# Scales of q and k taken from each job's own tiles, and the load of f issued first

## The chip, the cores and the metric

The kernel runs on one core of a Trainium2 chip. The metric is the device time of one execution in microseconds (us), lower is better. The unchanged kernel took 1197.27 us, the median of three runs that lay between 1194.51 and 1199.98 us.

## What is computed

The reference is an attention with a decay, followed by a feed-forward layer. The inputs are q, k, v of shape (8 batches, 8 heads, 576 positions, 64), f of shape (8, 8, 576), w_in of 512 x 2048 and w_out of 2048 x 512, all float32.

```python
scores = matmul(q, k.T) / sqrt(64)
cum = cumsum(log(clip(f, 1e-4, 1)), axis=-1)
scores = where(causal, -1e9, scores + cum[..., :, None] - cum[..., None, :])
attn = softmax(scores)                       # max subtracted, sum + 1e-9
x = matmul(attn, v)                          # laid out as 4608 tokens x 512
h = x @ w_in
g = where(h >= 1, h, where(h <= -1, 0, (h + 1) ** 2 / 4))
out = g @ w_out
```

## The kernel before

Float32 products are made of float16 ones: a value is scaled by a power of two and split into a high and a low float16 part, and three matmuls (high-high, high-low, low-high) stand for one product. The scale has to be known before the split, and it is taken from the largest absolute value of the data.

**Jobs.** The attention is cut into 36 jobs, numbered p = 0 to 35. A job is one batch and one pair of heads. Batch 0 is cut once more by rows, so jobs 0 to 3 are the first 256 positions of batch 0 and jobs 4 to 7 the rest; jobs 8 to 11 are batch 1, and so on, four jobs a batch. Jobs 0 to 11 score in float32, and jobs 12 to 35 (`NQK` is 12) score with the split of q and k. A job goes through these steps:

- `load` (L340) brings q and k of the pair into one of two float32 tiles `qk32` by DMA, two jobs ahead of their use.
- `load_decay` (L369) brings rows of the running sums of log f, `cum_d`, into `ck`.
- `prepare` (L379) makes the transposed q and k. For jobs from 12 on ScalarE (L389) and VectorE (L390) write the high and low parts `qs`, and one DMA transpose (L393) turns them into `qkT`.
- `scores` (L443) runs the score matmuls of one row block into the PSUM tile `s` (L466), and GpSimd (POOL) builds the decay term from `ck`, `nsig` and `cqs` (L474, L478).
- `weights` (L542) joins the two on VectorE (L556), runs the exponential on ScalarE (L560) and the normalisation and split on both (L574, L575), and transposes the result by DMA (L581).
- `values` (L588, L595) multiplies by v and writes the batch's x (L605); jobs 0 to 7 use `early_values` (L529, L537).

**Feed-forward units.** There are 18 chunks of 256 tokens times 8 blocks of the hidden layer, 144 units. A unit is `moe_front` (matmuls L637, then ScalarE and VectorE L646 to L651) and `moe_back` (matmuls L665). A unit can run when its tokens are finished. The main loop deals the units that are ready over the row blocks of the next jobs; what is left at the end runs by itself.

**Weights.** `weight_load` and `weight_split` (L177, L189) bring the feed-forward weights in and split them, among jobs 1 to 6. The split is mostly VectorE work (L196, L199, L202, L228).

**Scales.** `across(dst, m)` (L111) spreads the largest value over all partitions: a PE transpose of the 128 x n tile into `s` (L119), three VectorE operations (L121, L122, L126), a small PE matmul with ones (L129) and a copy back (L130). `scale_of` (L105) makes the power of two with three VectorE operations (L107, L101, L109). The PSUM tile `s` has one buffer, which the score matmuls and `across` share.

- `value_scale(b)` (L236) reads v of a batch a second time, four DMAs on POOL's queue into the tile `vm` (two buffers), each followed by a VectorE maximum (L245), then one `across`.
- `query_scale(b)` (L261) does the same for q and k of a batch: eight DMAs of 288 KB on POOL's queue (L268) into the same two `vm` buffers, eight maxima (L269), one `across`, and then `nsig`, `nalpha` and `cqs` (L278 to L284). It is called for batches 2 to 7, six times.

**What sets the order.** Instructions are recorded in the order of the program, and a scheduler then puts them into the five engines' queues by what it takes to be ready. Each queue runs strictly in its order. Work whose inputs are there early, such as the maxima of `query_scale`, is moved far ahead of the place where it is written: the 48 loads of `query_scale` stand in the trace between 18.5 and 371.8 us.

**Start.** `load(0)`, then `decay_sums` (L140): the load of f (L143), the logarithm, the running sum, its store to `cum_d` (L153), from which the `ck` rows are loaded (L372).

Of the kernel before, what the change touches and what calls it, by code (L numbers as in the profile page):

```python
# [8 lines left out]
F32 = mybir.dt.float32  # L9
# [6 lines left out]
P = 128  # L16
# [14 lines left out]
NQK = 12  # L31
# [14 lines left out]
def kernel(  # L46
# [90 lines left out]
    cum_d = dram.tile([B * H, S], F32, name="cum_d")  # L137
    cq8 = const.tile([P, NT5, B * H], F32, name="cq8")

    def decay_sums():  # L140
        fl = early
        nb = B * H
        nc.sync.dma_start(fl[0:nb, 0:S], f.rearrange("b h s -> (b h) s"))  # L143
# [112 lines left out]
    sqk = const.tile([P, 2, B], F32, name="sqk")  # L256
    nsig = const.tile([P, B], F32, name="nsig")
    nalpha = const.tile([P, B], F32, name="nalpha")
    cqs = [const.tile([P, NT5, H], F32, name=f"cqs{i}") for i in range(2)]

    def query_scale(b):  # L261

        ms = tiny.tile([P, 2, NPAIR], F32, name="m8", bufs=2)
        for j, src in enumerate((q, k)):
            for i in range(NPAIR):
                st = two.tile([P, S], F32, name="vm")
                part = src[b, 2 * i:2 * i + 2].rearrange("h s d -> (h s d)").rearrange("(p n) -> p n", p=P)
                nc.gpsimd.dma_start(st, part)  # L268
                nc.vector.tensor_reduce(  # L269
                    out=ms[:, j, i:i + 1], in_=st, axis=AX.X, op=ALU.max, apply_absolute_value=True  # L270
                )
        m2 = tiny.tile([P, 2], F32, name="m2q", bufs=2)
        nc.vector.tensor_reduce(out=m2, in_=ms, axis=AX.X, op=ALU.max)
        mk = tiny.tile([P, 2], F32, name="mk", bufs=2)
        across(mk, m2)
        sc = sqk[:, :, b]
        scale_of(sc, mk, mk)
        nc.vector.tensor_scalar(  # L278
            out=nsig[:, b:b + 1], in0=sc[:, 0:1], scalar1=sc[:, 1:2], scalar2=-8.0, op0=ALU.mult, op1=ALU.mult
        )  # L280
        nc.vector.reciprocal(nalpha[:, b:b + 1], nsig[:, b:b + 1])
        nc.vector.tensor_scalar(
            out=cqs[b % 2], in0=cq8[:, :, b * H:(b + 1) * H], scalar1=nsig[:, b:b + 1], scalar2=-0.125,
            op0=ALU.mult, op1=ALU.mult,  # L284
        )

    early_z = const.tile([P, 5, NB], F32, name="early_z")

    class Scales:
# [89 lines left out]
    def prepare(w):  # L379

        t_ = two.tile([P, 2, 2, SP], F16, name="qkT")
        if w.p >= NQK:
            w.nsig, w.nalpha = nsig[:, w.b:w.b + 1], nalpha[:, w.b:w.b + 1]
            w.cqs = cqs[w.b % 2][:, :, 2 * w.hp:2 * w.hp + 2]
            w.qk = [(t_[:, 0, lq], t_[:, 1, lk]) for lq, lk in ((0, 0), (0, 1), (1, 0))]
            qs = one.tile([P, 2, 2, SP], F16, name="qs")
            for j in range(2):
                sc = sqk[:, j, w.b:w.b + 1]
# [348 lines left out]
    for p in range(njobs + 1):  # L737
# [3 lines left out]
        if w:  # L741
# [82 lines left out]
```

## Time and profile before

| | |
|---|---|
| time, median of 3 | 1197.27 us |
| the profiled execution | 1195.69 us |
| its span, first to last instruction | 1193.9 us |
| mean granted TensorE clock | 0.951 |
| PE (TensorE matmul) busy | 1064.8 us, 89% |
| DVE (VectorE) busy | 806.8 us, 68% |
| ACT (ScalarE) busy | 770.4 us, 65% |
| POOL (GpSimd) busy | 476.1 us, 40% |

The profile is of one execution. PEld is the load of matmul weights. The page gives the busy time of each engine over the whole span; other views give the same for any stretch of it, list the instructions of an engine in order of time with the idle time before each and what ended it, and add up the waits between pairs of lines. A row of a timeline reads: start in us, duration in us, engine, line, operation, output and inputs, shapes, count, and in brackets the idle time before it and the releaser. Instructions on an engine's own sequencer that only issue DMAs carry a q (SPq).

### The profile page before, as it was taken

The numbers are of one execution on the slowest core, as the hardware profiler recorded it, in microseconds if no ns is written. First come the engines' busy times: TensorE is split into PE (matmuls) and PEld (weight loads), VectorE is DVE, ScalarE is ACT, GpSimd is POOL, SyncE is SP. The second block draws the span as 40 slices with busy tenths as digits, with TensorE's granted clock in tenths as the row PEclk, the third lists the DMA queues.
The fourth block names the chain that finished last, engine by engine and source line by source line (L and its number), as shares of the span: only waits on it lengthen the run. The fifth ranks groups of instructions, "written<-read, shape, count | busy, mean of one in ns | idle before, by whom it ended". The sixth has DMA issues, their size and how long they took to land. (4 is left out here: it accounts for less than half of the span.)

```text
span 1193.9 us, 24608 instructions
## 1 busy us (share of the span) xinstructions
PE 1064.8 (89%) x8871; PEld 681.6 (57%) x8871; DVE 806.8 (68%) x2140; ACT 770.4 (65%) x1599; POOL 476.1 (40%) x811
## 2 busy tenths in 40 slices
PE   2566766998689899999999999999999999999998
PEld 1334443655356556655666665565566666677665
DVE  5979878777778777768656666777767866522222
ACT  2756555758567767777667666786777776644443
POOL 3588643534464544544432232454434444000000
PEclk9767888999789999999999999999999999999999
DMA  8797744689989977867665555777767773300000
GB/s 269 220 296 210 216 138 143 134 192 162 181 159 201 188 132 161 153 137 147 123 115 103 108 111 116 149 157 139 141 129 146 128 130 66 74 19 2 19 18 18
DMA packets 392537, 162.60 MB, mean 136 GB/s; under 512 B 370016, under 2 KB 371040, under 8 KB 392416
## 3 DMA queue, kind: packets, MB, share of 16 engines
q1 hardware_dynamic: 377312, 115.03, 49.4%
q0 software_dynamic: 9920, 36.58, 10.8%
q10 hardware_dynamic: 5184, 9.44, 2.3%
q8 instruction: 69, 1.13, 0.4%
q14 instruction: 52, 0.43, 0.1%
HBM read 89.80 MB, written 9.58 MB: 83 GB/s over the span
## 5 line engine op out<-in xcount | busy, mean ns | idle before, releaser
L637 PE MATMUL ph<-x,place 128*128 128x256 f16 (+3 forms) x4608 | 430.3, 248 | 10.1 <-DVE u L648 8.0
L665 PE MATMUL po<-place,g 128*128 128x512 f16 x1728 | 412.8, 382 | 4.1 <-ACT g L650 3.9
L637 PEld LDWEIGHTS <-place 128*128 128x128 f16 x4608 | 355.4, 99 | 85.4 <-issue 29.2
L474 POOL TENSOR_SCALAR sdr<-ck,nsig,cqs 128x128 f32<-128x128 f32 (+1 forms) x192 | 154.3, 808 | 297.7 <-DVE pr L575 278.5
L665 PEld LDWEIGHTS <-g 128*128 128x128 f16 x1728 | 162.3, 98 | 176.9 <-issue 8.3
L560 ACT ACTIVATE sdr<-sdr,nm 128x128 f32<-128x128 f32 (+1 forms) x240 | 132.6, 553 | 75.8 <-DVE nm L556 75.1
L648 DVE SCALAR_TENSOR_TENSOR u<-ph,z,u 128x512 f32<-128x512 f32 x136 | 101.5, 746 | 107.0 <-ACT u L647 106.7
L646 ACT ACTIVATE u<-ph,z 128x512 f32<-128x512 f32 x136 | 104.4, 768 | 80.0 <-PE ph L637 78.1
L650 ACT ACTIVATE g<-u,z 128x512 f16<-128x512 f32 x136 | 97.8, 719 | 71.0 <-DVE u L648 67.1
L575 DVE SCALAR_TENSOR_TENSOR pr<-sdr,rc,pr 128x128 f16<-128x128 f32 (+1 forms) x224 | 116.3, 555 | 39.9 <-ACT pr L574 37.7
L651 DVE SCALAR_TENSOR_TENSOR g<-u,z,g 128x512 f16<-128x512 f32 x136 | 104.2, 766 | 48.1 <-ACT g L650 47.6
L574 ACT ACTIVATE pr<-sdr,rc 128x128 f16<-128x128 f32 (+1 forms) x224 | 112.6, 550 | 18.9 <-ACT sdr L560 14.3
L556 DVE CUSTOM_DVE_ANT_0 sdr<-s,sdr,nalpha 128x128 f32<-128x128 f32 (+1 forms) x192 | 98.4, 546 | 26.5 <-PE s L466 16.2
L466 PE MATMUL s<-qkT 64*128 64x128 f16 (+5 forms) x704 | 88.3, 347 | 26.7 <-DVE nm L556 23.9
L595 PE MATMUL big<-pT,vs 128*64 128x64 f16 (+3 forms) x1008 | 83.8, 291 | 18.6 <-DMA pT<-pr 10.8
L647 ACT ACTIVATE u<-u 128x512 f32<-128x512 f32 x144 | 89.8, 624 | 2.5
L478 POOL TENSOR_SCALAR_AFFINE_SELECT sdr<-sdr 128x128 f32<-128x128 f32 x240 | 85.0, 363 | 7.8
L595 PEld LDWEIGHTS <-vs 128*64 128x64 f16 x1008 | 53.1, 113 | 51.6 <-issue 33.2
L474 POOL TENSOR_SCALAR sd<-ck,nsig,cqs 64x576 f32<-64x576 f32 x48 | 47.0, 980 | 78.9 <-DMA ck<-cum_d 60.5
L466 PEld LDWEIGHTS <-qkT 64*128 64x128 f16 (+1 forms) x864 | 32.8, 99 | 59.7 <-issue 46.1
L390 DVE SCALAR_TENSOR_TENSOR qs<-qk,sqk,qs 128x640 f16<-128x640 f32 x48 | 42.4, 910 | 30.8 <-ACT qs L389 30.8
L389 ACT ACTIVATE qs<-qk,sqk 128x640 f16<-128x640 f32 x48 | 37.3, 820 | 38.8 <-DMA qkT<-qs 33.2
(163 smaller groups left out, 1140.3 us busy)
## 6 DMA issues: line engine op xcount, KB each, us to landing
ck<-cum_d POOLq DMA_DIRECT2D x48, 288.0 KB, 4.5
out_dram<-ot ACTq DMA_DIRECT2D x36, 256.0 KB, 3.5
qk<-in_k_dram SPq DMA_DIRECT2D x64, 128.0 KB, 3.1
vm<-in_v_dram POOLq DMA_DIRECT2D x28, 288.0 KB, 3.5
v<-in_v_dram SPq DMA_DIRECT2D x56, 128.0 KB, 3.0
qk<-in_q_dram SPq DMA_DIRECT2D x56, 128.0 KB, 2.8
vm<-in_q_dram POOLq DMA_DIRECT2D x24, 288.0 KB, 3.4
vm<-in_k_dram POOLq DMA_DIRECT2D x24, 288.0 KB, 3.4
```

What stands on the lines that cost most here:

```text
L466: nc.tensor.matmul(outs[h][:, c0:c1], lhsT=x[rows], rhs=y[rows, c0:c1], start=(i == 0), stop=(i == len(terms) - 1),)
L474: nc.gpsimd.tensor_scalar(out=sd[p0:p1, 0:wid], in0=w.ck[h][p0:p1, 0:wid], scalar1=w.nsig if w.p < NQK else w.nsig[p0:p1], scalar2=w.cqs[p ...
L556: nc.vector.tensor_tensor_reduce(out=a, in0=sp, in1=a, scale=w.nalpha, scalar=BIG, op0=ALU.add, op1=ALU.min, accum_out=nm[:, i:i + 1],)
L560: nc.scalar.activation(a, a, AF.Exp, bias=nm[:, i:i + 1], scale=-1.0, accum_out=sm[:, i:i + 1])
L574: nc.scalar.activation(pr[:, :, 0, i, :], a, AF.Copy, scale=rc[:, i:i + 1])
L575: nc.vector.scalar_tensor_tensor(out=pr[:, :, 1, i, :], in0=a, scalar=rc[:, i:i + 1], in1=pr[:, :, 0, i, :], op0=ALU.mult, op1=ALU.subtract,)
L595: nc.tensor.matmul(av[64 * h:64 * h + 64, at + s0:at + s1], lhsT=w.vs[:, vl, h, t, :], rhs=w.pT[:, t, pl, h, s0:s1], start=(t == 0 and pi ...
L637: nc.tensor.matmul(ph[:, fi, a0:a1], lhsT=wi[fb][:, wl, t, fi * P:(fi + 1) * P], rhs=xs[b][:, t, xl, s0:s0 + a1 - a0], start=(fi == 0 and ...
L646: nc.scalar.activation(u, h, AF.Relu, scale=z.u[:, i:i + 1], bias=z.h[:, i:i + 1])
L648: nc.vector.scalar_tensor_tensor(out=u, in0=h, scalar=z.t[:, i:i + 1], in1=u, op0=ALU.max, op1=ALU.min)
L651: nc.vector.scalar_tensor_tensor(out=g[:, 1], in0=u, scalar=z.r[:, i:i + 1], in1=g[:, 0], op0=ALU.mult, op1=ALU.subtract)
L665: nc.tensor.matmul(po[ch][i], lhsT=g[:, gl, fi * TC + i * P:fi * TC + (i + 1) * P], rhs=wo[fb][:, wl, fi, :], start=(first and fi == 0 and ...
```

## The change

`query_scale` is gone with its loads, and so are the per-batch tiles `sqk`, `nsig`, `nalpha` and `cqs`. Each job from 12 on now takes its own scales in `prepare`: two VectorE maxima over the job's own `qk32` tile (128 x 640 each, q and k), one `across`, one `scale_of`, then `nsig`, `nalpha` and `cqs` for the pair of heads. That is 24 times where `query_scale` ran six times, so `across` runs 40 times in the program instead of 22. The load of f moves from `decay_sums` to the front of the program.

```diff
+    nc.sync.dma_start(early[0:B * H, 0:S], f.rearrange("b h s -> (b h) s"))
+
     def decay_sums():
         fl = early
         nb = B * H
-        nc.sync.dma_start(fl[0:nb, 0:S], f.rearrange("b h s -> (b h) s"))
...
-    def query_scale(b):
-        ms = tiny.tile([P, 2, NPAIR], F32, name="m8", bufs=2)
-        for j, src in enumerate((q, k)):
-            for i in range(NPAIR):
-                st = two.tile([P, S], F32, name="vm")
...
-                nc.gpsimd.dma_start(st, part)
-                nc.vector.tensor_reduce(
-                    out=ms[:, j, i:i + 1], in_=st, axis=AX.X, op=ALU.max, apply_absolute_value=True
-                )
...
         if w.p >= NQK:
-            w.nsig, w.nalpha = nsig[:, w.b:w.b + 1], nalpha[:, w.b:w.b + 1]
-            w.cqs = cqs[w.b % 2][:, :, 2 * w.hp:2 * w.hp + 2]
+            m2 = tiny.tile([P, 2], F32, name="m2q", bufs=2)
+            for j in range(2):
+                nc.vector.tensor_reduce(
+                    out=m2[:, j:j + 1], in_=w.x32[j], axis=AX.X, op=ALU.max, apply_absolute_value=True
+                )
+            mk = tiny.tile([P, 2], F32, name="mk", bufs=2)
+            across(mk, m2)
+            sc2 = tiny.tile([P, 2], F32, name="sc2", bufs=2)
+            scale_of(sc2, mk, mk)
+            bh = w.b * H + 2 * w.hp
+            w.nsig = tiny.tile([P, 1], F32, name="nsig", bufs=3)
+            nc.vector.tensor_scalar(
+                out=w.nsig, in0=sc2[:, 0:1], scalar1=sc2[:, 1:2], scalar2=-8.0, op0=ALU.mult, op1=ALU.mult
+            )
+            w.nalpha = tiny.tile([P, 1], F32, name="nalpha", bufs=3)
+            nc.vector.reciprocal(w.nalpha, w.nsig)
+            w.cqs = tiny.tile([P, NT5, 2], F32, name="cqs", bufs=3)
+            nc.vector.tensor_scalar(
+                out=w.cqs, in0=cq8[:, :, bh:bh + 2], scalar1=w.nsig, scalar2=-0.125, op0=ALU.mult, op1=ALU.mult
+            )
...
-                if r == w.r0 and w.hp == 1 and w.b + 1 < B and p + 3 >= NQK:
-                    query_scale(w.b + 1)
```

How the queues' contents stand, at three places (line numbers are those of the kernel shown in the rows, so one source line has two numbers).

SP's queue at the start of the program, before (the two loads of q for job 0 stand ahead of these rows). `qk_0` and `qk_1` are the two q and k tiles, x is the scratch tile that holds f and its sums, place a raw block of weights.

```order
L362 DMA qk_0_119<-in_k_dram 128x2x64 x2
L143 DMA x<-in_f_dram 64x576
L362 DMA qk_1_120<-in_q_dram 128x2x64 x2
L362 DMA qk_1_120<-in_k_dram 128x2x64 x2
L244 DMA x<-in_v_dram 128x576 x3
L153 DMA cum_d<-x 64x576
L244 DMA x<-in_v_dram 128x576
L424 DMA vs<-in_v_dram 128x2x64 x2
L362 DMA qk_0_119<-in_q_dram 128x2x64 x2
L362 DMA qk_0_119<-in_k_dram 128x2x64 x2
L185 DMA place_100<-in_moe_w_in_dram 128x2x512
L372 DMA ck<-cum_d 128x256 x3
```

The same place after the change:

```order
L140 DMA x<-in_f_dram 64x576
L332 DMA qk_0_115<-in_q_dram 128x2x64 x2
L332 DMA qk_0_115<-in_k_dram 128x2x64 x2
L332 DMA qk_1_116<-in_q_dram 128x2x64 x2
L332 DMA qk_1_116<-in_k_dram 128x2x64
L154 DMA cum_d<-x 64x576
L332 DMA qk_1_116<-in_k_dram 128x2x64
L245 DMA x<-in_v_dram 128x576 x3
L342 DMA ck<-cum_d 128x256 x2
```

The load of f stands first instead of fifth, the store of the sums is the ninth issue instead of the thirteenth, and four issues stand between that store and the first loads of `ck`, where there were eight.

DVE's queue while the last block of weights is split (`place` is a raw weight tile, `u` scratch), before:

```order
L228 SCALAR_TENSOR_TENSOR place_103<-place_105,sw,place_103 128x512
L269 TENSOR_REDUCE m_5265<-vm 128x1 x3
L196 TENSOR_SCALAR u<-place_106 128x512
L269 TENSOR_REDUCE m_5265<-vm 128x1
L199 SCALAR_TENSOR_TENSOR u<-place_106,u 128x512
L648 SCALAR_TENSOR_TENSOR u<-ph,early_z,u 128x512
L202 SCALAR_TENSOR_TENSOR place_106<-place_106,u 128x512
L269 TENSOR_REDUCE m_5265<-vm 128x1
L196 TENSOR_SCALAR u<-x 128x512
```

The same split after the change:

```order
L229 SCALAR_TENSOR_TENSOR place_104<-place_106,sw,place_104 128x512
L551 TENSOR_SCALAR rc<-sm_1405 128x2
L552 RECIPROCAL rc<-rc 128x2
L551 TENSOR_SCALAR rc<-sm_1428 128x1
L552 RECIPROCAL rc<-rc 128x1
L197 TENSOR_SCALAR u<-place_107 128x512
L200 SCALAR_TENSOR_TENSOR u<-place_107,u 128x512
L203 SCALAR_TENSOR_TENSOR place_107<-place_107,u 128x512
L636 SCALAR_TENSOR_TENSOR u<-ph,early_z,u 128x512
L197 TENSOR_SCALAR u<-x 128x512
```

Five maxima of q and k that stood before and among the steps of the split are gone, and nothing stands in their place.

DVE's queue in a late job, before, where the split of q and k for the next job stands (`top` and `mv` here belong to the scale of v, `qs` to the split):

```order
L121 TENSOR_REDUCE top_6561<-s_6559 1x1
L249 TENSOR_REDUCE m1_10461<-m4_10448 128x1
L568 TENSOR_SCALAR rc_6642<-sm2_6639 128x1
L122 TENSOR_SCALAR top_6561<-top_6561 1x1
L571 RECIPROCAL rc_6642<-rc_6642 128x1
L126 TENSOR_SCALAR dg_6564<-ident_81,top_6561 1x1
L575 SCALAR_TENSOR_TENSOR pr3_6578<-sdr_2_124,rc_6585,pr3_6578 128x4x128
L575 SCALAR_TENSOR_TENSOR pr3_6578<-sdr_3_125,rc_6585,pr3_6578 128x4x128
L575 SCALAR_TENSOR_TENSOR pr4_6637<-sd4_1_127,rc_6642,pr4_6637 128x5x128
L390 SCALAR_TENSOR_TENSOR qs_7099<-qk32_0_119,sqk_113,qs_7099 128x640
```

A late job after the change:

```order
L126 TENSOR_SCALAR dg_6785<-ident_81,top_6782 2x2
L593 SCALAR_TENSOR_TENSOR x_4847<-big_6851,x_4847 128x576
L420 SCALAR_TENSOR_TENSOR vs_7068<-v32_117,sv_113,vs_7068 128x640
L130 COPY mk_6779<-s_6780 128x2
L107 TENSOR_SCALAR mk_6779<-mk_6779 128x2
L101 TENSOR_SCALAR mk_6779<-mk_6779 128x2
L109 RECIPROCAL sc2_6789<-mk_6779 128x2
L364 TENSOR_SCALAR nsig_6793<-sc2_6789 128x1
L368 RECIPROCAL nalpha_6795<-nsig_6793 128x1
L370 TENSOR_SCALAR cqs_6797<-cq8_89,nsig_6793 128x10
L378 SCALAR_TENSOR_TENSOR qs_6799<-qk32_1_116,sc2_6789,qs_6799 128x640 x2
```

The split `qs` of every such job now stands behind the copy out of `s` (L130) and the six small operations that follow from it.

More of the change, by code (lines that the diff above doesn't have):

```diff
@@ L254, in value_scale @@
         scale_of(sv[:, b:b + 1], pv[:, b:b + 1], m)
[L256 to L259, printed above, removed]
-    def query_scale(b):
-        ms = tiny.tile([P, 2, NPAIR], F32, name="m8", bufs=2)
-        for j, src in enumerate((q, k)):
-            for i in range(NPAIR):
-                st = two.tile([P, S], F32, name="vm")
-                part = src[b, 2 * i:2 * i + 2].rearrange("h s d -> (h s d)").rearrange("(p n) -> p n", p=P)
-                nc.gpsimd.dma_start(st, part)
-                nc.vector.tensor_reduce(
-                    out=ms[:, j, i:i + 1], in_=st, axis=AX.X, op=ALU.max, apply_absolute_value=True
-                )
[L272 to L285, printed above, removed]
     early_z = const.tile([P, 5, NB], F32, name="early_z")
```

2 lines of the change are left out of this document (1 added, 1 removed).

## The prediction

> **What bounds the kernel now.** I first cut the span into stretches and read the engines' busy time in each, then asked what the busiest engine of the early stretches waits for, then looked at single rows. The columns are the stretch, its length, busy us (and instructions) of PE, PEld, DVE, ACT and POOL, the granted TensorE clock, the busy share of the DMA engines and GB/s.
>
> ```profile
> 0.00:20.00 20.00, 5.93 (x22) 3.14 (x22) 8.70 (x20) 3.50 (x6) 5.59 (x20) 1.00 0.78 212
> 20.00:90.00 70.00, 36.42 (x155) 23.43 (x155) 56.70 (x168) 44.13 (x121) 48.14 (x71) 0.73 0.89 276
> 90.00:210.00 120.00, 82.16 (x478) 54.74 (x478) 99.79 (x289) 68.38 (x154) 67.79 (x98) 0.82 0.60 176
> 210.00:243.00 33.00, 32.70 (x228) 19.55 (x230) 24.69 (x67) 24.43 (x59) 16.54 (x32) 1.00 0.64 137
> 243.00:450.00 207.00, 178.98 (x1519) 111.47 (x1516) 159.17 (x447) 138.63 (x298) 99.82 (x181) 0.93 0.87 174
> 450.00:1045.00 595.00, 584.26 (x5300) 370.41 (x5298) 416.36 (x1098) 428.34 (x874) 238.25 (x412) 1.00 0.66 126
> 1045.00:1190.00 145.00, 144.32 (x1178) 98.84 (x1176) 41.38 (x56) 62.45 (x90) 0.00 (x0) 1.00 0.03 12
> ```
>
> From 450 us on PE is 98% to 99.5% busy: that part is as long as its matmuls. The last 145 us are feed-forward units alone, so attention ends with work in store and an attention job that comes late there costs nothing by itself. PE's idle time lies early: 86 us before 210 us, 28 us from 243 to 450. Whatever shortens the early part arrives sooner at a PE-bound rest, and the end moves by as much; whatever adds PE work later is paid in full.
>
> In 90 to 210 us DVE is busy 99.8 of 120 us, more than PE. These are its idle times there (us, times, longest), then the maxima of q and k that it runs:
>
> ```profile
> DVE m L269 <- DMA vm<-in_q_dram: 6.8, 5, 3.0
> DVE m L245 <- DMA vm<-in_v_dram: 3.3, 5, 1.6
> DVE m L269 <- DMA vm<-in_k_dram: 1.6, 4, 0.7
> ```
>
> ```profile
> 20.00:90.00 70.00, 4.41 (x6) 0.73 0.89 276
> 90.00:210.00 120.00, 19.33 (x26) 0.82 0.60 176
> 243.00:390.00 147.00, 11.79 (x16) 0.92 0.88 177
> ```
>
> So of 120 us DVE spends 19.3 us on these maxima and stands 8.4 us before them waiting for their loads. With the 3.3 us for v it is busy or held by a `vm` load for 111.5 us, 93%. What is queued behind shows on DVE and then on POOL:
>
> ```profile
> 164.29 0.75 DVE L269 TENSOR_REDUCE m<-vm 128x1 f32<-128x576 f32 x1 [1.12 <-DMA vm<-in_q_dram]
> 168.02 0.75 DVE L269 TENSOR_REDUCE m<-vm 128x1 f32<-128x576 f32 x1 [2.98 <-DMA vm<-in_q_dram]
> 168.69 0.42 DVE L196 TENSOR_SCALAR u<-place 128x512 int32<-128x512 int32 x1
> ```
>
> ```profile
> 169.07 0.55 POOL L268 DMA_DIRECT2D vm<-in_k_dram  x1 [3.18 <-DVE m L269]
> 169.70 1.59 POOL L474 TENSOR_SCALAR sdr<-ck,cq 128x256 f32<-128x256 f32 x2
> ```
>
> The split of weights (L196) stands behind the maxima, and POOL, which must wait for the buffer that DVE is to free, issues the next load before it may build the decay term (L474) of the running job. The two queues hold each other.
>
> **Part 1: f first.** SP's issues and the first long wait of PE:
>
> ```profile
> 0.75 0.97 SPq L362 DMA_DIRECT2D qk<-in_q_dram  x2
> 2.79 0.57 SPq L143 DMA_DIRECT2D x<-in_f_dram  x1
> 10.24 0.48 SPq L153 DMA_DIRECT2D cum_d<-x  x1
> 14.96 1.42 SPq L372 DMA_DIRECT2D ck<-cum_d  x3
> ```
>
> ```profile
> 28.11 1.23 PE L466 MATMUL s<-qkT 64*128 64x256 f32 x4 [8.96 <-DVE nm L556]
> ```
>
> f is issued 2.79 - 0.75 = 2.0 us earlier, so the store of the sums comes at about 8.2 us. Four issues instead of eight follow before `ck`, at some half a microsecond each, so `ck` goes out near 10.6 us instead of 14.96, 4.4 us earlier. PE's 9 us wait hangs on it (ck, POOL, L556). It costs four loads of q and k half a microsecond each, hidden by the same wait. I take -3 us, between 0 (DVE's weight work sets the pace from 20 us on) and -4.4.
>
> **Part 2: 20 to 90 us.** Six maxima, 4.4 us, go; with freed buffers the loads of v move up (in the queues 13 maxima of v precede the end of job 3, against 8), which gives back 5 x 0.74 = 3.7 us of DVE. POOL's blocking remains in part. I take -2, between 0 and -4.4.
>
> **Part 3: 90 to 210 us.** DVE's own work falls from 99.8 to 80.5 us, with the waits for v 83.8. How long the stretch becomes depends on how full DVE can be kept. At the 93% of now: 90.2 us, a gain of 29.8. At the 81% (56.7 of 70) of the stretch 20 to 90: 103.5, gain 16.5. At the 75% (24.7 of 33) of 210 to 243: 112, gain 8. PE's 82.2 us fit below all three. I take -16.5, because 20 to 90 us has the same work (weight splits, float32 jobs) with few of the maxima.
>
> **Part 4: 243 to 450 us.** Here 16 maxima, 11.8 us, go and jobs 12 to 16 get their own scales. The DVE rows for that:
>
> ```profile
> L269 DVE TENSOR_REDUCE m<-vm 128x1 f32<-128x576 f32 x48 | 35.5, 742 | 12.9 <-DMA vm<-in_q_dram 10.5 <-DMA vm<-in_k_dram 2.3
> L121 DVE TENSOR_REDUCE top<-s 2x1 f32<-2x128 f32 (+1 forms) x22 | 6.0, 271 | 2.0 <-PE s L119 2.0
> L122 DVE TENSOR_SCALAR top<-top 2x1 f32<-2x1 f32 (+1 forms) x22 | 3.0, 135 | 0.1
> ```
>
> A job gets two maxima of 640 instead of 576 elements, 2 x 742 x 640/576 = 1.65 us, and ten small operations of 135 to 271 ns, 1.35 to 2.7 us; with 0.19 each 1.9. Together 3.5 us per job, 84 us for 24 jobs. Five jobs are 17.5 us, against 11.8 us removed and about 4 us for two of the six old chains of small operations (the old transposes stand at 243, 351, 465, 577, 731 and 847 us): no net change. I take 0, from -5 (POOL no longer blocked) to +5 (`s` held longer).
>
> **Part 5: PE work.** `across` runs 18 more times. The old ones for q and k, and how PE passes one of them in the full stretch (the transpose, the next row, the small matmul, the next row):
>
> ```profile
> L119 PE MATMUL s<-ident,m2q x6: 270/272/273, 242.5 to 846.5; 128*2 128x128 f32 x6
> ```
>
> ```profile
> 731.27 0.27 PE L119 MATMUL s<-ident,m2q 128*2 128x128 f32 x1
> 731.38 1.15 PE L637 MATMUL ph<-x,place 128*128 128x256 f16 x9
> ...
> 736.46 0.38 PE L129 MATMUL s<-dg,ones 2*128 2x2 f32 x2
> 736.77 1.38 PE L637 MATMUL ph<-x,place 128*128 128x256 f16 x11
> ```
>
> From start to start it costs 0.11 + 0.31 = 0.42 us; PE works on between the two halves. 18 x 0.42 = 7.6 us. The upper end is the sum of the durations, 18 x 0.65 = 11.7. Since PE is the bound from 243 us on, I add +7.6.
>
> **Part 6: waits.** Behind the waiting L119 and L129 stand the units' matmuls in PE's queue, and behind the copy L130 the split `qs` of the next job and the g of the units in DVE's. What PE waited in 450 to 1045 us for an `across`, and for DVE in the units:
>
> ```profile
> PE ph L637 <- DVE mv L130: 0.5, 1, 0.5
> PE ph L637 <- DVE u L648: 6.7, 5, 2.7
> ```
>
> 0.5 us, once, is nothing. But DVE gets 19 jobs x 3.5 = 66 us more there, less about 8 for four old chains: 416 + 58 = 474 of 595, 80% where it was 70%. How PE's idle share goes with DVE's load:
>
> ```profile
> 600.00:750.00 150.00, 148.99 (x1240) 93.75 (x1237) 95.30 (x251) 101.19 (x201) 45.92 (x88) 1.00 0.60 114
> 750.00:930.00 180.00, 174.49 (x1553) 110.09 (x1551) 134.63 (x363) 133.41 (x278) 83.44 (x138) 0.99 0.74 141
> ```
>
> From 64% to 75% of DVE, PE's idle share goes from 0.7% to 3.1%: 0.21 points per point, so ten points more would be 2.1% of 595 = 12.6 us. If only the 6.7 us grow with the load, it is 1 us. I take +5, nearer to the waits counted than to a slope through two stretches that differ in other things too.
>
> **Sum.** -3 - 2 - 16.5 + 0 + 7.6 + 5 = -8.9 us. The profiled execution took 1195.69 us, 1.8 over its span and 1.6 below the median of 1197.27. From the median that is 1188.4, rounded to **1188 us**.
>
> **Rivals.**
>
> *The maxima were only filler (0.22).* They stand where the scheduler saw DVE free. For it: they have no deadline before job 12. Against it: the rows at 164 to 168 us, where work that is ready stands behind them. Then part 3 returns only the 8.4 us of waits and parts 1 and 2 nothing: -8.4 + 12.6 = +4.2, 1201.5 us. That would be a change that moves the waits and not the end.
>
> *DVE comes late in the full stretch (0.16): slower.* The place is 450 to 1045 us: ten small operations and two maxima per job delay L648 and L651, and PE, with two PSUM buffers for the units, waits. It decides from 20 us of added idle time (3.4% of that stretch), where it has eaten -21.5 + 7.6. The stretch 243 to 450 shows 77% of DVE with PE idle for 28 of 207 us, 13.5%; half way between that and the 3.1% above is 8.3%, against 1.8% now: 6.5% of 595 = 39 us in place of 5. Sum +25, 1222 us. Against it: PE waits for DVE only 6.7 us there now. What could stretch the small operations is this, from a row of the early part and from the old `query_scale`:
>
> ```profile
> 122.67 1.64 DVE L101 TENSOR_SCALAR mp<-mp 128x2 int32<-128x2 int32 x1
> L101 DVE TENSOR_SCALAR mk<-mk x6: 160/170/253, 252.3 to 850.6; 128x2 int32<-128x2 int32 x6
> ```
>
> One such operation was held to 1.64 us; six later ones had a median of 170 ns and none exceeded 253. The Trainium skill, page "SBUF — State Buffer", section "SBUF: two separate sides", says that VectorE and GpSimd share a pair of ports by an exclusive lock, and that the loser is blocked for the other's whole instruction; this speaks against a change that puts ten small VectorE operations per job beside GpSimd's decay terms. By that rule as a steady cost the sum would be this rival's; the six later rows do not bear it out, the early one does.
>
> *DVE stays as full as now (0.14): a larger gain.* Part 3 returns 29.8 us, the rest as forecast: -22.2, 1175 us.
>
> **Chances and range.** The forecast has 0.48. About 0.5% (6 us) is what a measurement can tell from no change. Of the forecast's own spread, some -18 to -2 us, six parts in seven lie beyond -6: 0.41 faster, 0.07 same. With the larger gain faster is 0.55; the filler case gives 0.16 same and 0.06 slower; the late DVE 0.16 slower. So 0.55, 0.23, 0.22. Parts 1 to 4 at their high ends and 5 and 6 as forecast lead to 1166 us, which needs all at once; the range begins at 1172, just under the larger gain. Upward it takes in the filler case with 3 us more of PE work, 1205. Left out are most of the late DVE and a little below, less than 0.2. The forecast's own range is 1179 to 1195.
>
> **What would show it.** Right: DVE without a `vm` wait for q and k, the stretch up to job 7's end (L537 at 223 us before) about 20 us shorter, PE's busy time up by 8 to 12 us, PE's idle time down by some 17. Wrong: the end of job 7 near 215 us or later with DVE idle for ACT or PE (filler); or PE's waits for L648 and L651 after 450 us tripled (late DVE); or `across` rows with PE standing idle before L129, which would void part 5.

## The result and the profile after

| | before | after |
|---|---|---|
| median of six runs each on one chip | 1198.24 us (1194.51 to 1200.09) | 1210.66 us (1209.12 to 1213.79) |
| ratio | | 1.0118, 95% interval 1.0097 to 1.014 |
| the profiled execution | 1195.69 us, span 1193.9 | 1209.12 us, span 1207.4 |
| busy PE / DVE, whole span | 1064.8 / 806.8 us | 1078.4 / 834.2 us |

The kernel became slower by 1.2%; the forecast was 1188 us with a range up to 1205. Lines have moved: the maxima of q and k are L355, the loads of q and k L332 and L336, the split L377 and L378, the scores L454, the joining of scores and decay L544, the units L625, L636 and L653.

The stretches of the changed kernel, columns as in the prediction:

```profile
20.00:90.00 70.00, 45.39 (x185) 28.86 (x184) 61.67 (x184) 47.96 (x134) 47.77 (x64) 0.88 0.95 286
90.00:210.00 120.00, 92.86 (x578) 59.02 (x578) 87.23 (x270) 75.88 (x169) 60.70 (x87) 0.87 0.44 116
...
243.00:450.00 207.00, 178.31 (x1569) 111.77 (x1568) 153.63 (x443) 131.02 (x274) 86.38 (x149) 0.94 0.68 137
450.00:1045.00 595.00, 565.64 (x5059) 357.98 (x5058) 446.16 (x1255) 412.83 (x853) 242.85 (x407) 0.99 0.64 124
```

Early, PE does more in the same time (45.4 for 36.4 us, 92.9 for 82.2). Later it does less: 565.6 for 584.3 us between 450 and 1045, while DVE has 446 us of work where it had 416. So the early gain came, and something after it took more than the gain. Over the whole span PE's busy time is 13.6 us up, and its idle time is what it was (1193.9 - 1064.8 = 129.1 us before, 1207.4 - 1078.4 = 129.0 after): what was saved early stands idle again later.

Where the two cross is read from the last write of each job. These rows give, for before, the starts of those of jobs 4 to 7 (L537) and 8 to 35 (L605), first and last:

```profile
L537 DVE SCALAR_TENSOR_TENSOR x<-big,sv,x x4: 531/546/551, 114.9 to 223.1; 128x320 f16<-128x320 f32 x4
L605 DVE SCALAR_TENSOR_TENSOR x<-big,x x28: 707/757/759, 246.8 to 1042.8; 128x576 f16<-128x576 f32 x28
```

The same two of the changed kernel:

```profile
L525 DVE SCALAR_TENSOR_TENSOR x<-big,sv,x x4: 536/543/550, 98.3 to 200.3; 128x320 f16<-128x320 f32 x4
L593 DVE SCALAR_TENSOR_TENSOR x<-big,x x28: 737/757/758, 229.0 to 1058.0; 128x576 f16<-128x576 f32 x28
```

Job 7 ends 22.8 us earlier (200.3 for 223.1), job 35 15.2 us later (1058.0 for 1042.8). From job 7 to job 35 the changed kernel needs 857.7 us where 819.7 were enough: 38 us are lost there.

What is new there is this, the maxima of q and k on DVE and what DVE stood idle for just ahead of them:

```profile
L355 DVE TENSOR_REDUCE m2q<-qk x48: 801/820/822, 218.3 to 962.0; 128x1 f32<-128x640 f32 x48
its engine sat idle before it (us, times) until:
  DMA qk<-in_q_dram: 33.8, 19
  DMA qk<-in_k_dram: 24.6, 14
```

DVE stands still for 58.4 us in 33 places because the q or k that it is to reduce has not landed (7.5 us more in four places count as "issue"). One such place, on SP's queue first (start, duration, line, operation):

```profile
858.46 1.11 SPq L332 DMA_DIRECT2D qk<-in_q_dram  x2
859.67 3.86 SPq L381 DMA_TRANSPOSE qkT<-qs  x1
863.59 0.62 SPq L336 DMA_DIRECT2D qk<-in_q_dram  x1
864.43 2.56 SPq L569 DMA_TRANSPOSE pT<-pr  x2
867.04 1.70 SPq L332 DMA_DIRECT2D qk<-in_k_dram  x2
868.78 1.52 SPq L336 DMA_DIRECT2D qk<-in_k_dram  x1
```

and the same time on DVE:

```profile
857.45 0.88 DVE L378 SCALAR_TENSOR_TENSOR qs<-qk,sc,qs 128x640 f16<-128x640 f32 x1
...
865.96 0.82 DVE L355 TENSOR_REDUCE m2q<-qk 128x1 f32<-128x640 f32 x1 [0.98 <-DMA qk<-in_q_dram]
...
874.46 0.82 DVE L355 TENSOR_REDUCE m2q<-qk 128x1 f32<-128x640 f32 x1 [3.34 <-DMA qk<-in_k_dram]
```

The split of job n (the row at 857.45 is its second half) frees the buffer; SP then issues the loads of job n+2 into it, but with DMA transposes between their parts, so the last part of k goes out at 868.78. DVE has the maxima of job n+2 about 15 instructions behind the split, comes to them too early, and stands still. Nothing needs those maxima yet: the scale chain of job n+2 runs a job later. What does need DVE stands behind them, here the joining of scores and decay, and PE waits:

```profile
873.17 0.83 PE L625 MATMUL ph<-x,place 128*128 128x64 f16 x12
876.60 0.22 PE L583 MATMUL big<-pT,vs 128*64 128x64 f16 x2 [2.60 <-DVE nm L544]
```

The three longest waits of PE for DVE between 450 and 1045 us (us, times, longest), where before had 6.7 us for the units' first operation on DVE and nothing else for DVE above 0.5:

```profile
PE ph L625 <- DVE u L636: 6.8, 7, 2.2
PE s L454 <- DVE nm L544: 4.8, 6, 1.5
PE big L583 <- DVE nm L544: 3.9, 2, 2.6
```

The first is as long as before, the other two are new. PE's idle time there rose from 10.7 us (595 - 584.26) to 29.4 us (595 - 565.64). From 243 to 450 us it is 28.7 us for 28.0, but made up differently: the wait for the units' first operation on DVE, before and then after, has grown tenfold.

```profile
PE ph L637 <- DVE u L648: 1.2, 3, 0.5
```

```profile
PE ph L625 <- DVE u L636: 12.6, 5, 6.1
```

### The profile page after: what moved, and what is told of

Same layout as the page of the kernel before. It is cut to its first block, busy times and chain, and to the rows that moved or that the text cites. A ratio compares the mean times of both kernels' runs of the same rounds, so it can differ in the third digit from the quotient of the medians.

```text
span 1207.4 us, 24776 instructions
## 1 busy us (share of the span) xinstructions
PE 1078.4 (89%) x8925; PEld 688.3 (57%) x8925; DVE 834.2 (69%) x2314; ACT 769.4 (64%) x1599; POOL 460.5 (38%) x763
## 5 line engine op out<-in xcount | busy, mean ns | idle before, releaser
L625 PE MATMUL ph<-x,place 128*128 128x256 f16 (+3 forms) x4608 | 444.7, 249 | 22.2 <-DVE u L636 19.4
L653 PE MATMUL po<-place,g 128*128 128x512 f16 x1728 | 422.5, 384 | 8.7 <-ACT g L638 5.6
L625 PEld LDWEIGHTS <-place 128*128 128x128 f16 x4608 | 359.2, 99 | 111.2 <-issue 34.8
L653 PEld LDWEIGHTS <-g 128*128 128x128 f16 x1728 | 161.6, 99 | 176.8 <-issue 15.4
L462 POOL TENSOR_SCALAR sdr<-ck,nsig,cqs 128x128 f32<-128x128 f32 (+1 forms) x192 | 150.8, 789 | 255.3 <-DVE pr L563 239.7
L636 DVE SCALAR_TENSOR_TENSOR u<-ph,z,u 128x512 f32<-128x512 f32 x136 | 101.3, 745 | 92.3 <-ACT u L635 91.8
L563 DVE SCALAR_TENSOR_TENSOR pr<-sdr,rc,pr 128x128 f16<-128x128 f32 (+1 forms) x224 | 119.9, 566 | 26.6 <-ACT pr L562 25.5
L639 DVE SCALAR_TENSOR_TENSOR g<-u,z,g 128x512 f16<-128x512 f32 x136 | 103.5, 761 | 45.4 <-ACT g L638 45.0
L462 POOL TENSOR_SCALAR sd<-ck,nsig,cqs 64x576 f32<-64x576 f32 x48 | 51.5, 1073 | 171.7 <-issue 55.8
L454 PE MATMUL s<-qkT 64*128 64x128 f16 (+5 forms) x704 | 88.3, 352 | 24.9 <-DVE nm L544 21.6
L544 DVE CUSTOM_DVE_ANT_0 sdr<-s,sdr,nalpha 128x128 f32<-128x128 f32 (+1 forms) x192 | 98.3, 544 | 6.3 <-PE s L454 4.8
L583 PE MATMUL big<-pT,vs 128*64 128x64 f16 (+3 forms) x1008 | 80.1, 281 | 11.7 <-DMA pT<-pr 6.3
L355 DVE TENSOR_REDUCE m2q<-qk 128x1 f32<-128x640 f32 x48 | 39.2, 818 | 66.1 <-DMA qk<-in_q_dram 33.8
L454 PEld LDWEIGHTS <-qkT 64*128 64x128 f16 (+1 forms) x864 | 32.9, 99 | 54.2 <-issue 37.5
L462 POOL TENSOR_SCALAR sdr<-ck,cq 128x128 f32<-128x128 f32 (+3 forms) x48 | 33.7, 701 | 44.7 <-DVE pr L563 30.3
```

The lines of the kernel that those rows point to most:

```text
L454: nc.tensor.matmul(outs[h][:, c0:c1], lhsT=x[rows], rhs=y[rows, c0:c1], start=(i == 0), stop=(i == len(terms) - 1),)
L462: nc.gpsimd.tensor_scalar(out=sd[p0:p1, 0:wid], in0=w.ck[h][p0:p1, 0:wid], scalar1=w.nsig if w.p < NQK else w.nsig[p0:p1], scalar2=w.cqs[p ...
L544: nc.vector.tensor_tensor_reduce(out=a, in0=sp, in1=a, scale=w.nalpha, scalar=BIG, op0=ALU.add, op1=ALU.min, accum_out=nm[:, i:i + 1],)
L563: nc.vector.scalar_tensor_tensor(out=pr[:, :, 1, i, :], in0=a, scalar=rc[:, i:i + 1], in1=pr[:, :, 0, i, :], op0=ALU.mult, op1=ALU.subtract,)
L583: nc.tensor.matmul(av[64 * h:64 * h + 64, at + s0:at + s1], lhsT=w.vs[:, vl, h, t, :], rhs=w.pT[:, t, pl, h, s0:s1], start=(t == 0 and pi ...
L625: nc.tensor.matmul(ph[:, fi, a0:a1], lhsT=wi[fb][:, wl, t, fi * P:(fi + 1) * P], rhs=xs[b][:, t, xl, s0:s0 + a1 - a0], start=(fi == 0 and ...
```

## The experiments

Theories: **1**, the maxima stand in DVE's in-order queue ahead of the landing of their loads, and what is behind them pays. **2**, it is the work that DVE was given. **3**, the 18 more maxima across the partitions (`across`) hold the `s` buffers and PE. **4**, for the load of f, that it costs or gains elsewhere. "The wait" below is DVE's idle time ahead of those reductions until q or k landed, 58.4 us in the changed kernel. Intervals are of the ratio to the kernel before on the same chip.

**Late maxima.** Maxima and scales share one tile with a single buffer:

```diff
-            m2 = tiny.tile([P, 2], F32, name="m2q", bufs=2)
+            ms4 = tiny.tile([P, 4], F32, name="m2q", bufs=1)
+            m2 = ms4[:, 0:2]
...
-            sc2 = tiny.tile([P, 2], F32, name="sc2", bufs=2)
+            sc2 = ms4[:, 2:4]
```

> The changed kernel with one edit: a job's two maxima and its two scales share one tile with a single buffer, so the maxima of a job can't start before the split of the job before has read its scales. On DVE's queue the maxima of job n+1 now stand behind the split of job n, where the changed kernel had those of job n+2 there; the work is the same. Theory 1 (the maxima stand in DVE's queue before their loads have landed, 66 us of standing still at line 355): DVE's waits on q and k loads at the maxima fall below 20 us, TensorE's waits for DVE between 243 and 1045 us fall, and the time falls by 10 to 30 us to 1180 to 1200, below the kernel before or equal to it. Theory 2 (it is the added busy time of the maxima and small operations, which is unchanged): 1205 to 1216, as the changed kernel. Theory 3 (the 18 more maxima across the partitions hold the two s buffers and TensorE): 1205 to 1216 too, perhaps slower, as the small chain now starts later for its split.

1157.71 us, ratio 0.9648 (0.9616 to 0.9679): 41 us faster than before, 53 us faster than the changed kernel, with the same work, and more than theory 1 had asked for. The maxima, two stretches, and the jobs' last writes of that kernel:

```profile
L356 DVE TENSOR_REDUCE m2q<-qk x48: 789/809/822, 218.4 to 924.7; 128x1 f32<-128x640 f32 x48
...
  DMA qk<-in_q_dram: 1.8, 1
```

```profile
243.00:450.00 207.00, 196.28 (x1816) 123.81 (x1815) 168.48 (x486) 145.67 (x305) 95.42 (x158) 0.97 0.74 146
450.00:1045.00 595.00, 588.65 (x5284) 376.72 (x5282) 451.17 (x1236) 421.15 (x857) 238.28 (x399) 1.00 0.64 123
```

```profile
L594 DVE SCALAR_TENSOR_TENSOR x<-big,x x28: 743/757/758, 229.2 to 1006.1; 128x576 f16<-128x576 f32 x28
```

The wait is gone (1.8 us for 58.4), PE is busy 196.3 and 588.7 us where it was 178.3 and 565.6, and DVE does more per time than in the changed kernel (451 for 446 us). Theories 2 and 3 fall as causes of the loss: work and `across` are all still there. Of the 51.2 us between the two profiled spans (1207.4 and 1156.2) 40.4 are idle time of PE. The other 10.8 are busy time of PE for the same number of matmuls; why those took longer is not shown.

**Short maxima.** `in_=w.x32[j]` becomes `in_=w.x32[j][:, 0:D]`, so a maximum reads 64 of 640 columns.

> The changed kernel with each maximum taken over the first 64 columns of its tile alone (it leaves most of the data out of the maximum); the maxima still read the tiles after their loads, and keep about their place on DVE's queue. Busy time of line 355 falls from 39 us to under 12 us. Theory 1 (waiting for the loads): the wait at line 355 stays above 40 us and the time stays within 8 us of the changed kernel, 1200 to 1212. Theory 2 (busy time): 27 us or more of DVE's work gone from jobs that are bound there, 1183 to 1198. Theory 3 (across): 1205 to 1213, no change.

1178.68 us, ratio 0.9834 (0.98 to 0.9869), just below theory 2's interval. Its wait, from the waits of DVE:

```profile
DVE m2q L355 <- DMA qk<-in_k_dram: 39.8, 24, 3.1
DVE m2q L355 <- DMA qk<-in_q_dram: 11.6, 16, 2.1
```

This is a miss of theory 1 as it was written: with 51.4 us of wait left, 32 us came back when DVE's work fell by 28 us (806.4 busy for 834.2). So standing still is not priced alone; it costs less when DVE has less to do behind it.

**No maxima.** `m2` is a constant tile of 20; the chain of each job stays.

> The changed kernel without the maxima: the scale chain of each job is kept, maximum across the partitions with its two transposes included, but is fed by a constant of 20, so it waits for no load (and the order may place it earlier). Theory 1: neither waits nor busy time of line 355 are left, 1172 to 1192, 20 to 40 us below the changed kernel. Theory 2: 1180 to 1198, about as the kernel with short maxima. Theory 3 (18 more maxima across): all of these are still there, so 1203 to 1213.

1150.07 us, ratio 0.9589 (0.956 to 0.9618): faster than all three expected, and farthest from theory 3's. Beside late maxima it shows what 37 us of maxima cost where they wait for nothing: 7.6 us, no more than the arrangement of the instructions alone can make (see **Neither** below).

**The load of f alone**, in the kernel before (the issue moved to the front of the program).

> The kernel before with only the load of f put first in the program; scales and second loads of q and k as before. The prediction's first part: -3 us (0 to -4.4), so 1193.8 to 1198.2. If the early load of f costs something elsewhere (theory 4: a part of the 12 us comes from it): above 1200.

1192.11 us, ratio 0.9942 (0.9919 to 0.9965): 6.8 us faster, beyond both expectations on the good side. It has no part in the loss.

**The wait without the work.** Late maxima, and at the changed kernel's place two small reductions that nothing reads:

```diff
+            pb = tiny.tile([P, 2], F32, name="pb", bufs=2)
+            for j in range(2):
+                nc.vector.tensor_reduce(
+                    out=pb[:, j:j + 1], in_=w.x32[j].rearrange("p (a d) -> p a d", d=D)[:, :, 0:1], axis=AX.XY, op=ALU.max
+                )
```

> The kernel with late maxima, to which two small reductions per job are added that nothing reads: each takes 8 or 10 numbers per partition from all the landed parts of a q or k tile. They stand on DVE's queue where the changed kernel's maxima stood (those of job n+2 within some 10 rows of the split of job n), so they bring back the wait for the loads with next to no busy time. Theory 1 (the wait costs it): DVE stands still over 40 us at the new line, and the time returns to 1190 to 1212. Theory 2 (what cost time was the busy work of the maxima at that early place): 48 small operations of some 0.1 to 0.2 us, up to 10 us, so 1158 to 1168.

1188.94 us, ratio 0.9919 (0.9888 to 0.9949): 31 us slower than late maxima. The new line:

```profile
L355 DVE TENSOR_REDUCE pb<-qk x48: 141/169/173, 215.8 to 935.5; 128x1 f32<-128x10 f32 x48
...
  DMA qk<-in_q_dram: 32.7, 16
  DMA qk<-in_k_dram: 17.8, 14
```

48 x 0.169 = 8 us of work, 50.5 us of wait, 31 us of time. The wait itself is shown as a cause, though at 1 us below the lower end of what theory 1 expected; 22 of the 53 us were still unexplained.

**The sizes exchanged.** As the last, but the unread reductions take whole tiles and the late ones, which feed the scales, 64 columns.

> The probe kernel with the sizes exchanged: the reductions that nothing reads, at the changed kernel's early place, take whole tiles (0.82 us each), and the late maxima that feed the scales take 64 columns (0.22 us each; they leave most of the data out of the maximum). DVE's work is 10 us above that of the changed kernel, its order nearly the same. If the long reductions behind the wait make the other 22 us: 1203 to 1222, waits over 50 us. If standing still alone counts, whatever follows it: 1184 to 1198, as the kernel with the small probe. If it is the scale chain that reads maxima of that place: 1184 to 1198 too.

1204.61 us, ratio 1.004 (1.0018 to 1.0062), 47 us slower than late maxima:

```profile
L355 DVE TENSOR_REDUCE pb<-qk x48: 798/820/821, 216.9 to 959.6; 128x1 f32<-128x640 f32 x48
...
  DMA qk<-in_q_dram: 39.2, 21
  DMA qk<-in_k_dram: 24.4, 13
```

Here nothing depends on the early reductions, the chain is fed late, and 47 of the 53 us are back. So it is wait and long operation together at a place where other work is due. How much of the step from 31 to 47 us comes from the longer operations and how much from 13 us more of wait is not parted: no run has long operations at the early place without a wait. The last 6 us lie within what small changes of the order do here (about 10 us, see **Neither** below).

**Three buffers for q and k.**

```diff
-                st = two.tile([P, S], F32, name="vm")
+                st = two.tile([P, S], F32, name="vm", bufs=1)
...
-    qk32 = [const.tile([P, 2, 2, NT5, D], F32, name=f"qk32_{i}") for i in range(2)]
+    qk32 = [const.tile([P, 2, 2, NT5, D], F32, name=f"qk32_{i}") for i in range(3)]
...
-        flat = qk32[ji % 2].rearrange("p j h t d -> p (j h t d)")
+        flat = qk32[ji % 3].rearrange("p j h t d -> p (j h t d)")
...
-            if NQK <= ji < NQK + 2:
+            if NQK <= ji < NQK + 3:
```

> The changed kernel with three buffers for q and k in place of two, the loads still issued two jobs ahead; to make room the buffer for the maxima of v is single in place of double. A load no longer waits for the split of two jobs before, and on DVE's queue the maxima of a job stand just ahead of its own scale chain, a job later than in the changed kernel. Theory 1: waits for q and k at line 355 below 15 us, 1150 to 1172, as with late maxima, though the edit is another (up to 8 us more if the single buffer for v costs). Theory 2 (work): 1203 to 1214, since the work is the same.

1158.41 us, ratio 0.9662 (0.9631 to 0.9694), as theory 1 said, but the expectation had the edit wrong in two points. The scheduler sends loads as early as buffers allow, so they now run three jobs ahead and still wait for a split, that of job n for the load of n+3. And the maxima of n+3 stand not just before their own chain but at that of job n+1, some 30 to 70 instructions behind the split of job n, since the two-buffer tile of the maxima must first be read by that chain. SP and then DVE in that kernel:

```profile
853.64 0.62 SPq L336 DMA_DIRECT2D qk<-in_k_dram  x1
```

```profile
843.20 0.88 DVE L378 SCALAR_TENSOR_TENSOR qs<-qk,sc,qs 128x640 f16<-128x640 f32 x1
...
860.82 1.52 DVE L355 TENSOR_REDUCE m2q<-qk 128x1 f32<-128x640 f32 x2
```

The last load goes out 10.4 us behind the start of the split's second half (853.64 - 843.20), nearly as late as in the changed kernel (868.78 - 857.45 = 11.3). Only, DVE comes to the maxima 7 us after that issue. The wait is 2.1 us in all. The maxima lie two jobs ahead of their use, and no cost of that can be told.

**Three buffers, maxima early again.** They are written out behind the preparation of the job before, into three buffers:

```diff
+    def maxima(w):
+        w.m2 = tiny.tile([P, 2], F32, name="m2q", bufs=3)
...
                 prepare(nxt)
+                if p + 2 < njobs and p + 2 >= NQK:
+                    maxima(pairs[p + 2])
```

> As the kernel with three buffers, but the maxima of job n+2 are written out right behind the preparation of job n+1, which puts them back at the changed kernel's place on DVE's queue, some 5 to 10 rows behind the split of job n. The loads' place on SP's queue stays; only their wait for the split is gone. If the loads come late because of the two buffers, the waits at the maxima fall below 20 us, and theory 1 says 1155 to 1172, theory 2 (work at an early place costs by itself) 1180 or more. If they come late because SP's queue stands behind the DMA transposes of the weights, the waits stay above 40 us, and theory 1 says 1190 to 1212.

1213.94 us, ratio 1.013 (1.0101 to 1.0159).

```profile
L352 DVE TENSOR_REDUCE m2q<-qk x48: 797/820/822, 193.9 to 938.5; 128x1 f32<-128x640 f32 x48
...
  DMA qk<-in_k_dram: 30.5, 14
  DMA qk<-in_q_dram: 28.3, 19
```

The expectation's question, buffers or SP's queue, is not answered, since the loads still wait for a split here. But beside the last kernel it is the cleanest pair: same buffers, same loads, same work, and the maxima of n+3 stand some 5 to 20 instructions behind the split of n in place of 30 to 70. That alone is 55 us, with 58.8 us of wait for 2.1.

**Late maxima and three buffers.**

> Late maxima and three buffers together. Theory 1: the wait is gone by either edit, so together they bring no more than one: 1152 to 1163. If waits of the loads for the splits also cost elsewhere: under 1150.

1163.24 us, ratio 0.9693 (0.9665 to 0.9722): no gain beyond either.

**Loads from ACT's queue.** The kernel with early maxima and three buffers; the loads of jobs 12 and later are issued by ACT (`eng = nc.scalar if ji >= NQK else nc.sync`), so that no DMA transpose stands between their parts.

> The kernel of three buffers with early maxima, but the loads of q and k for jobs 12 and later are issued from ACT's queue, within some ten rows of ACT's own split operations, in place of SP's queue behind the DMA transposes. The maxima stay at their early place on DVE, some ten rows behind the split. If SP's queue makes the loads late: the waits at the maxima fall below 30 us, and theory 1 says 1157 to 1185 (by 0.83 us of time per us of standing still, the ratio between the changed kernel and the one with late maxima; up to 10 us more if the issuing on ACT costs). If an early place alone costs: waits gone, but 1190 or more. If the loads land late for another reason (the DMA engines): waits over 50 us, 1195 to 1215.

1192.38 us, ratio 0.994 (0.9915 to 0.9965), 21.6 us below the same kernel with loads from SP.

```profile
DVE m2q L353 <- DMA qk<-in_q_dram: 18.6, 14, 3.7
DVE m2q L353 <- DMA qk<-in_k_dram: 13.7, 11, 2.0
```

The wait is 32.3 us for 58.8, a little over the 30 expected, so SP's queue makes somewhat under half of it (26.5 us). The rest would be the way from split to issue to landing, which DVE outruns; that way was not measured apart. The time is in the interval only with the 10 us left open for issuing on ACT, whose cost was not measured by itself.

**No `across`.** The maxima stay but are unread, and one constant scale serves all jobs.

> The changed kernel with the maxima kept but read by nothing; the scales come once from a constant of 20, so the 24 maxima across the partitions of jobs 12 and later and the small operations behind them are left out. The maxima keep their early place on DVE's queue. Theory 1: the waits at line 355 stay above 40 us, and 1185 to 1208 is left: what the chains take on DVE and PE (some 6 to 20 us) goes. Theory 3 (across and its chain cost the time): 1150 to 1170.

1174.63 us, ratio 0.9796 (0.9764 to 0.9828), between the two intervals. Its wait is 30.4 us for q and 7.4 for k, together 37.8 where over 40 was expected.

**Neither.** No maxima and no chains, one constant scale.

> The changed kernel with neither maxima nor chains for q and k: one constant scale for all jobs, set up once. It shows what q and k scales cost at all in this schedule, and the prediction's early gain by itself. Theory 1: no wait and no work, 1135 to 1152, at most 15 us below the kernel without maxima (1150.1). Theory 3: 20 us or more below it, under 1130.

1159.72 us, ratio 0.9664 (0.9634 to 0.9693), above both expectations, and 9.7 us slower than the kernel without maxima, which does more. So the chains, `across` included, cost nothing that can be told where nothing waits, and the arrangement of the instructions alone is worth about 10 us either way: smaller differences than that between these kernels are not read as effects. Beside it the unread maxima of the kernel without `across` cost 15 us, with 37.8 us of wait; the other 36 us up to the changed kernel come with the chains and 20.6 us more of wait, which this run doesn't part.

**Late maxima, f at its old place.**

> The kernel with late maxima, but the load of f at its old place, behind the loads of q and k of the first job. What the other half of the change is worth beside the first: if the load of f ahead brings the same as it did in the kernel before (6.8 us), 1162 to 1168; if it brings the prediction's 3 us, 1159 to 1162; if nothing is left of it later in the program, 1155 to 1159.

1164.41 us, ratio 0.9711 (0.9682 to 0.9741): f first is worth 6.7 us here (7.5 by the ratios, as the two kernels ran on different chips), 6.8 in the kernel before. Each alone is below the 10 us named above; that two kernels agree is what speaks for it.

**The wait put into the kernel before.** The same small unread reductions, nothing else changed.

> The kernel before, with the small probe reductions added for jobs 12 and later, that nothing reads; they stand on DVE's queue 10 to 20 rows behind the split of the job two before. All else, the second loads and the scales of q and k by batch included, is as before. Theory 1: DVE stands still 25 to 60 us at the new line, and the kernel is slower by 10 to 35 us, 1208 to 1233. If a wait of this kind costs only beside scale chains for each job: within 6 us of before, 1192 to 1204.

1216.47 us, ratio 1.0137 (1.0106 to 1.0167): 16.6 us slower, inside theory 1's interval.

```profile
L385 DVE TENSOR_REDUCE pb<-qk x48: 146/169/173, 244.8 to 930.1; 128x1 f32<-128x10 f32 x48
...
  DMA qk<-in_q_dram: 18.7, 14
  DMA qk<-in_k_dram: 16.0, 15
```

34.7 us of wait and 8 us of work, without any scale chain per job, make the kernel before as slow as the changed one (ratio 1.0137 beside 1.0118, with intervals that overlap).

All together, by the wait:

| kernel | wait, us | DVE busy, us | time, us |
|---|---|---|---|
| no maxima | 0 | 801.2 | 1150.1 |
| neither maxima nor chains | 0 | 768.6 | 1159.7 |
| late maxima | 1.8 | 837.3 | 1157.7 |
| three buffers | 2.1 | 836.5 | 1158.4 |
| late maxima and three buffers | 0 | 838.1 | 1163.2 |
| late maxima, f at its old place | 4.3 | 836.4 | 1164.4 |
| loads from ACT | 32.3 | 831.7 | 1192.4 |
| no `across` | 37.8 | 801.1 | 1174.6 |
| the small probe | 50.5 | 834.3 | 1188.9 |
| short maxima | 51.4 | 806.4 | 1178.7 |
| changed kernel | 58.4 | 834.2 | 1210.7 |
| three buffers, early maxima | 58.8 | 838.9 | 1213.9 |
| sizes exchanged | 63.6 | 838.7 | 1204.6 |

At about the same work (832 to 839 us) the time goes from 1158 to 1164 us at a wait of 0 to 4 us to 1189 to 1192 at 32 to 50 and 1205 to 1214 at 58 to 64, within these groups not in the order of the wait; with some 30 us less work like waits come out 10 to 18 us lower (short maxima beside the small probe, no `across` beside loads from ACT).

## Why the prediction was wrong, step by step

The change has three effects, each measured by itself: f first -6.8 us; the scales of each job from its own tiles, without the wait, another -34.4 us (1157.71 - 1192.11); the early place of the maxima, with its wait, +53.0 (1210.66 - 1157.71). From 1198.2 that gives 1210.

**Part 1** (f first, -3, at most -4.4): -6.8, beyond its bound. The store of the sums and the first `ck` went out earlier than the 8.2 and 10.6 us worked out, as SP's queue of the changed kernel shows:

```profile
6.47 0.49 SPq L154 DMA_DIRECT2D cum_d<-x  x1
...
9.17 0.85 SPq L342 DMA_DIRECT2D ck<-cum_d  x2
```

The gain goes beyond the bound only behind the first job: that one ends 4.4 us earlier in the kernel before (37.8 us for 42.2) and 2.9 us earlier with late maxima (38.1 for 41.0), the fourth 9.0 us (81.0 for 90.0) and 6.3 us (81.2 for 87.5). Why it grows there was not tried.

**Parts 2 and 3** (-2 and -16.5): part 3 right, part 2 not shown. The last writes of jobs 0 to 3 and 4 to 7 in the kernel before with f first, then of jobs 0 to 3 in the changed kernel:

```profile
L538 DVE SCALAR_TENSOR_TENSOR x<-po,sv,x x4: 462/468/479, 37.8 to 81.0; 128x256 f16<-128x256 f32 x4
L538 DVE SCALAR_TENSOR_TENSOR x<-big,sv,x x4: 516/534/540, 97.8 to 216.5; 128x320 f16<-128x320 f32 x4
```

```profile
L525 DVE SCALAR_TENSOR_TENSOR x<-po,sv,x x4: 461/466/480, 38.1 to 81.5; 128x256 f16<-128x256 f32 x4
```

With f first in both, job 3 ends no earlier (81.5 for 81.0), and from there to job 7's end it takes 118.8 us for 135.5: -16.7. With f behind in both (late maxima with f at its old place, beside before) job 3 ends at 87.45 us for 90.02, -2.6, and the rest takes 118.2 us (205.69 - 87.45) for 133.1 (223.08 - 90.02), -14.8. All in all the changed kernel's job 7 ends 22.8 us earlier, where 21.5 was forecast and about 20 given as the sign. So the maxima were not only filler, and the first rival falls.

**Parts 4 and 5** (0 and +7.6): too high. With late maxima the way from job 7 to job 35 takes 805.7 us (1006.1 - 200.4), 14.0 less than before's 819.7, with 24 chains for six. Most of it lies in part 4's stretch, where no net change was forecast: PE's idle time from 243 to 450 us is 10.7 us (207 - 196.28) for 28.0. PE's busy time rose by 2.8 us (1067.6 for 1064.8), and the kernel with no chains at all isn't faster. Of the signs named, PE's busy time up by 8 to 12 us and its idle time down by some 17, the changed kernel shows 13.6 us up and no change in idle time. Which of the things removed there (second loads, their maxima, POOL's issues and waits) gave the 14 us was not separated.

**Part 6** (waits, +5, 1 to 12.6) is the step that failed. It named what is queued behind the chain's transposes, its copy and the split, and read the price from waits that the kernel before already had. It left out the one new wait: a maximum can't start before its own q or k has landed. In the kernel before nothing on DVE needed q and k sooner than the split, a job later. The trace held the means to see it: loads that start when a split frees the buffer, behind DMA transposes on SP's queue. The instruction order held the rest: the maxima of n+2 about 15 rows behind the split of n. What it cost, with the work that then stands behind it, was 53 us, in place of 5. That the forecast was off by no more than 23 us is luck: part 1 came out 3.8 us and parts 4 and 5 together some 22 us better than forecast, and hid about half of the miss.

**The second rival** had the effect right: DVE late for PE in the full stretch, deciding "from 20 us of added idle time". Against before PE's idle time from 450 to 1045 us rose by 18.7 us, just short of that. Against late maxima, from 243 us on, it is 41 us more (58.1 for 17.1). Its mechanism was another, small operations that are held up. The operation it showed, in jobs 12 and later:

```profile
L101 DVE TENSOR_SCALAR mk<-mk x24: 161/169/347, 261.9 to 1001.2; 128x2 int32<-128x2 int32 x24
```

None of the 24 is near the 1.64 us of the early row; their median of 169 ns is that of the old six. The rule of the Trainium skill, page "SBUF — State Buffer", section "SBUF: two separate sides", as a steady cost of such operations is not borne out by this trace. The sign named for this rival, waits of PE for L648 and L651 tripled after 450 us, did not come either: 6.8 us for 6.7 at L648's operation, 1.7 for none at L651's. The growth to 12.6 us at the former lies before 450 us, with 18 us of what late maxima win back (196.28 - 178.31); the rest is spread over other waits.

**Open** remain why wait and work together cost more than the two added (31 us for the small probe, 7.6 for the late maxima, 53 for both), which no run takes apart, and how the wait divides between SP's queue and the plain way from split to landing, of which one run gives somewhat under half to the queue.

## What to carry to other kernels

When an operation is moved or added on an in-order queue, ask first when its inputs land on the chip, on which queue their load is issued and what stands before it there; a scheduler places the operation by its own idea of that time, and if it is too early, everything behind it waits although nobody needs its result yet. The remedy had no cost here that could be told: tie the operation to something that happens later, such as a single-buffered tile that the step before must read first. That small edit turned a loss of 1.2% into a gain of 3.5%.

## What was not expected of the hardware

The DMA transposes of q and k on SP's queue in the changed kernel, with the duration of one in ns, least, median and most:

```profile
L381 SPq DMA_TRANSPOSE qkT<-qs x24: 3032/3376/4428, 267.2 to 1005.4; - x24
```

A DMA transpose of q and k holds the queue for 3.4 us, some six times as long as the plain load at 858.46 us above (two in 1.11 us), and parts the pieces of one load. So the load whose buffer was free at 858 us was fully issued only at 870 us. And a plain load issued from ACT holds that engine's queue too, here for the q of the kernel with loads from ACT:

```profile
L333 ACTq DMA_DIRECT2D qk<-in_q_dram x48: 369/405/786, 188.6 to 901.8; - x48
```

Six issues per job, with medians of 0.4 us or more, are over 2.4 us of ACT in each.
